# An inner Strassen product in the first gate/up pass, joined W_down sums, and the second LayerNorm spread over more units

## The chip, the cores and the metric

The kernel runs on one core of one Trainium2 chip. The metric is the device time of one execution in microseconds; several executions are taken and the median is given, with the lowest and highest. Most executions of one kernel agree within 0.3%. A profile is one execution under the hardware profiler, and its span is about 1.8 us shorter than the time of the same run.

One warning for reading small differences. The first 44 us of a run hang on loads from memory, and in the profiles quoted here the point where TensorE starts its unbroken work (43.7 to 46.0 us) differs by over 2 us from run to run with the same code up to there. The change is of that size. So beside the times I use the **length of the first pass**, from its first matmul to the first matmul of the stage behind it, read in each profile.

## The reference, cut to what matters

```python
h  = x + A(layernorm(x), wqkv, wo)                  # linear attention, 2048 tokens, width 1024
h2 = h + B(layernorm(h), W_gate, W_up, W_down)
# B: F = 3584
gate = relu(x @ W_gate);  up = x @ W_up             # [2048,1024] @ [1024,3584]
return (gate * up) @ W_down                         # [2048,3584] @ [3584,1024]
```

## The kernel before

The second half runs twice, for 1024 tokens each time: a gate/up pass of 14 units, then the W_down product. A unit is one gate or one up block: 2 column blocks of W (u = 0, 1), each 256 wide, times all 1024 tokens. Products are added up in banks of PSUM (`ps` in the profile); to read a finished bank out is called an evacuation here. A unit is computed by a Strassen-Winograd scheme: of the 2x2 blocks of W and of the activations, seven products P1 to P7 instead of eight, each of four 128-row matmuls of 512 columns. Even units ("gate") end in relu, odd ones ("up") multiply into the gate's result. The sums of weight blocks (T1 to T4, "G") are made on VectorE, the copies from bank to bank ("fork": one product feeds two outputs) on ScalarE.

```python
def ffn_unit(n, fill, mid):                 # first pass
    ...
    def p1(u):
        prod(u, BA[u], w_blk(u, 0, 0), a_blk(0, 0), True, "P1")     # 4 matmuls of 512
        ident_act(bank(BB[u]), bank(BA[u]), ...)                     # fork 1, ScalarE
    def p2(u):
        prod(u, BA[u], w_blk(u, 1, 0), a_blk(1, 0), False, "P2")
        evac(0, 0, u, BA[u], "h11")
    p1(0); p1(1)
    fillin(1)                                # one of the weight sums of the next unit
    ... P5, P6, P2, P7, P3 ...
    for u in range(2):
        prod(u, BB[u], t_blk(u, 3), a_blk(1, 1), False, "P4")
        evac(0, 1, u, BB[u], "h21")
    if n < NPAIR - 2:
        load_w_next(); load_w_next()

def ffn_unit2(n, pre, wina, winb):          # second pass: P1 and P5 by an inner Strassen
    def sub(dst, bdst, w, x, start, name):   # one of seven small products
        for kk in range(2):
            mm(dst, w[0](kk), x[0](kk), ...)                         # 2 matmuls of 256
    ...

def wd_sums(q):                             # W_down sums: four of 128x512 for each of 14 row pairs
    add(0, wb(0, 1), wb(0, 0), ...); add(2, wb(1, 1), wb(0, 1), ...)
    add(1, wb(1, 1), wsum[:, k, 0, :], ...); add(3, wb(1, 0), wsum[:, k, 1, :], ...)

# end of the attention stage: weights of units 0 and 1 are loaded from its loop
    if t in (4, 5, 18, 19):
        load_w_next()
load_w_next(); load_w_next()                 # unit 2
```

The second LayerNorm of the later 1024 tokens (three ScalarE steps for each of eight tiles) is fitted into eight of the first pass's units, three steps a unit.

Of the kernel before, what the change touches and what calls it, by code (L numbers as in the profile page):

```python
# [132 lines left out]
def bass_sequential_preLN__linear_attn_block__glu_gated_reglu__prompt_kernel(  # L133
# [71 lines left out]
    with es:  # L205
# [105 lines left out]
        m5r = RW[:, (NWS - 3) * WDW:(NWS - 3) * WDW + 2 * SHB].bitcast(f32)  # L311
        sg_g = [RWG[:, x:x + 4 * WDW].bitcast(f16).rearrange("p (j m t) -> p j m t", j=4, t=SHB)
# [134 lines left out]
        B_m5r = _Buf("m5r")  # L447
        B_xr = bufs("xr_", 2)
# [73 lines left out]
        B_m5r.over = flat(B_wsum)  # L522
        for b_ in B_hnE:
            b_.over = B_o + B_oT
# [184 lines left out]
        def wd_sums(q):  # L709
            k = q % NWR  # L710

            def wb(r, h):
                return wraw[:, k, r, h * NW:(h + 1) * NW]

            def add(o, in0, in1, reads):
                PL.add("dve", lambda e: e.tensor_tensor(out=wsum[:, k, o, :], in0=in0, in1=in1, op=ALU.subtract),
                       reads=reads, writes=[B_wsum[k][o]], name="WT%d_%d" % (o, q))

            add(0, wb(0, 1), wb(0, 0), [B_wraw[k]])
            add(2, wb(1, 1), wb(0, 1), [B_wraw[k]])  # L720
            add(1, wb(1, 1), wsum[:, k, 0, :], [B_wraw[k], B_wsum[k][0]])
            add(3, wb(1, 0), wsum[:, k, 1, :], [B_wraw[k], B_wsum[k][1]])
            dma(sl_ws[k], t_v[:, q % 2, :, q // 2, :], wsum[:, k].rearrange("p o (h c) -> p (o h) c", c=HNW),
                "st_wt_%d" % q, reads=B_wsum[k], writes=[B_tscr[q]])
            dma(sl_rw[k], r_v[:, 0, 2 * (q % 2):2 * (q % 2) + 2, q // 2, :],
                wraw[:, k, 1, NW:2 * NW].rearrange("p (h c) -> p h c", c=HNW), "st_rw_%d" % q, reads=[B_wraw[k]],
                writes=[B_rscr[0][q]])

        def wl_sums(m):
            z = m % 2  # L730

            def wq_(k, h):
                return wsum[:, (2 * m + k) % NWR, :, h * HNW:(h + 1) * HNW], B_wsum[(2 * m + k) % NWR]

            def t(j):
                return lsum[:, :, j, :], [B_lsum[j]]

            def add(j, x, y):
                PL.add("dve", lambda e: e.tensor_tensor(out=lsum[:, :, j, :], in0=x[0], in1=y[0],
                                                        op=ALU.subtract),  # L740
                       reads=x[1] + y[1], writes=[B_lsum[j]], name="WL%d_%d" % (j, m))

            def half(i):
                if i == 0:
                    add(0, wq_(0, 1), wq_(0, 0))
                    add(2, wq_(1, 1), wq_(0, 1))
                else:
                    add(1, wq_(1, 1), t(0))
                    add(3, wq_(1, 0), t(1))
                    dma(sl_ls[0], l_v[:, 0:4, :, m, :], lsum, "st_wl_%d" % m, reads=B_lsum, writes=[B_lscr[m]])  # L750
            def wr(k, h):
                return wraw[:, (2 * m + k) % NWR, 1, NW + h * HNW:NW + (h + 1) * HNW], [B_wraw[(2 * m + k) % NWR]]

            def addw(j, x, y):
                PL.add("pool", lambda e: e.tensor_tensor(out=lsw[:, z, j, :], in0=x[0], in1=y[0], op=ALU.subtract),
                       deps=[PL.prog["pe"][-1]], reads=x[1] + y[1], writes=[B_lsw[z][j]], name="WM%d_%d" % (j, m))

            def t_(j):
                return lsw[:, z, j, :], [B_lsw[z][j]]

            def last():
                addw(3, wr(1, 0), t_(1))
                if m == NM - 1:
                    load_wd_next()
                    load_wd_next()
                dma(sl_lw[z], l_v[:, 4, :, m, :], lsw[:, z], "st_wm_%d" % m, reads=B_lsw[z], writes=[B_wscr[m]])
                for q in (2 * m + NWR, 2 * m + NWR + 1):
                    if q < NPAIR:
                        load_wraw(q)
            raw = [lambda: addw(0, wr(0, 1), wr(0, 0)), lambda: addw(2, wr(1, 1), wr(0, 1)),  # L770
                   lambda: addw(1, wr(1, 1), t_(0)), last]
            return [lambda: half(0), lambda: half(1), raw]

# [617 lines left out]
        def hh_sums(q):  # L1391
            f1, f2 = 2 * q, 2 * q + 1
            PL.add("dve", lambda e: e.tensor_tensor(out=D1[:, q, :], in0=hh[:, f1, SBW:2 * SBW],
                                                    in1=hh[:, f2, SBW:2 * SBW], op=ALU.add),
                   reads=[B_hh[f1][1], B_hh[f2][1]], writes=[B_D1[q]], name="D1_%d" % q)
            PL.add("dve", lambda e: e.tensor_tensor(out=hh16[:, f1, SBW:2 * SBW], in0=hh[:, f1, 0:SBW],
                                                    in1=hh[:, f1, SBW:2 * SBW], op=ALU.subtract),
                   reads=[B_hh[f1][0]], writes=[B_hh[f1][1]], name="D3_%d" % q)

# [11 lines left out]
        def w_inner1(n):  # L1411
            z = n % 2
            i = (2 * n) % NWG
# [11 lines left out]
            g = B_g1[z]  # L1425
# [6 lines left out]
        def x_inner(first=False):  # L1432
            xs, bxs = (xs1, B_xs1) if first else (xs5, B_xs5)
# [36 lines left out]
        def ffn_unit(n, fill, mid):  # L1470
            Lg = n * 2
            up = n % 2
            iw = [(Lg + u) % NWG for u in range(2)]
            kt = [(Lg + u) % NTR for u in range(2)]
            f0 = 2 * (n - up)
            BA, BE, BB, BC_ = [0, 1], [2, 3], [4, 5], [6, 7]
            if up:
                BB, BC_ = BC_, BB

            def H(k, t, u):  # L1480
                return hh[:, f0 + 2 * u + k, t * SBW:(t + 1) * SBW], B_hh[f0 + 2 * u + k][t]

            def H2(k, t):
                return hh[:, f0 + k:f0 + k + 3:2, t * SBW:(t + 1) * SBW], [B_hh[f0 + k][t], B_hh[f0 + 2 + k][t]]

            def fillin(n_):
                for _ in range(n_):
                    if fill:
                        fill.pop(0)()

            def go(fs):
                for f_ in fs:
                    f_()

            def a_blk(k, t):
                return (lambda kk: hnT[:, k * KH + kk, t * SBW:(t + 1) * SBW]), B_hnT[t * STB:(t + 1) * STB]

            def s_blk(i):
                return (lambda kk: Ssum[:, i, kk, :]), [B_S[i]]

            def w_blk(u, k, h):
                return (lambda kk: wring[:, iw[u], k * KH + kk, h * P:(h + 1) * P]), [B_w[iw[u]]]

            def t_blk(u, j):
                return (lambda kk: Tring[:, kt[u], j, kk, :]), [B_T[kt[u]][j]]

            def prod(u, b, st_, mov, start, name):
                (sf, sr), (mf, mr) = st_, mov
                for kk in range(KH):
                    mm(bank(b), sf(kk), mf(kk), start and kk == 0, kk == KH - 1, sr + mr, B_bank[b],  # L1510
                       "%s%s_0_%d" % (name, "gu"[up], n), skip=True)

            def evac5(k, t, u, src, bsrc, tmp, btmp, name):
                d, db = (tmp[:, u, :], btmp[u]) if up else H(k, t, u)
                PL.add("dve", lambda e: e.tensor_tensor(out=d, in0=src, in1=ftmp[:, u, :], op=ALU.add),
                       reads=[bsrc, B_s5[u]], writes=[db], name=name)

            def fin5(k, t, tmp, btmp, name):
                d, db = H2(k, t)
                if up:  # L1520
                    PL.add("dve", lambda e: e.tensor_tensor(out=d, in0=d, in1=tmp, op=ALU.mult), reads=btmp, writes=db,
                           name=name)
                else:
                    PL.add("act", lambda e: e.activation(out=d, in_=d, func=ACTF.Relu), reads=[], writes=db, name=name)

            def evac(k, t, u, b, name):
                d, db = H(k, t, u)
                if up:
                    PL.add("dve", lambda e: e.tensor_tensor(out=d, in0=bank(b), in1=d, op=ALU.mult),
                           reads=[B_bank[b]], writes=[db], name=name)  # L1530
                else:
                    ident_act(d, bank(b), [B_bank[b]], [db], name, func=ACTF.Relu)

            def p1(u):
                prod(u, BA[u], w_blk(u, 0, 0), a_blk(0, 0), True, "P1")
# [53 lines left out]
        def ffn_unit2(n, pre, wina, winb):  # L1589
# [127 lines left out]
            if n > 0:  # L1717
                p2()
# [788 lines left out]
```

## Time and profile before

| | before |
|---|---|
| time, median (lowest to highest) | 719.08 us (719.01 to 719.67) |
| profile span | 717.7 us |
| first gate/up pass | 227.18 to 396.39 = 169.21 us |
| period of a first-pass unit | 12.087 us, 56 matmuls |
| period of a second-pass unit | 11.69 us, 40 matmuls of 512 and 28 of 256 |

TensorE is the bound throughout, at full clock, and the first pass has no gap: 784 matmuls x 0.21583 us are the 169.21 us.

### The profile page before, as it was taken

What the parts mean: (1) busy time and instruction counts of PE and PEld (TensorE: products, weight loads), DVE (VectorE), ACT (ScalarE), POOL (GpSimd) and SP (SyncE); (2) the same over time, 40 slices, a digit from 0 to 9 for tenths busy, and PEclk for the clock granted to TensorE, in tenths of its full rate; (3) what the DMA queues carried; (4) which work ended last, traced back from release to release, by engine and by line L of the source; (5) the groups of instructions that cost most, each with busy time, mean ns of one, the idle gap of its engine ahead of it and who ended that gap; (6) DMA issues with size and microseconds to landing.
All of it is one profiled execution on the core that took longest, in us unless ns stands there. A gap on an engine that the chain in (4) does not pass through costs nothing.

```text
span 717.7 us, 13021 instructions
## 1 busy us (share of the span) xinstructions
PE 708.3 (99%) x4923; PEld 387.4 (54%) x4979; DVE 597.5 (83%) x1010; ACT 384.1 (54%) x679; POOL 109.1 (15%) x178
## 2 busy tenths in 40 slices
PE   9999999999999999999999999999999999999998
PEld 4344444444444444444444568865555555547887
DVE  6988867799776889889888787888888888988885
ACT  4877666764841456687756102036766667643010
POOL 3221100000360103422321002320000000000331
PEclk9999999999999999999999999999999999999999
DMA  9843244015998797999999999995343534267996
GB/s 296 260 86 92 38 128 162 13 31 97 209 217 243 236 273 233 275 310 304 298 276 268 308 265 310 321 243 155 96 132 105 160 101 135 82 203 246 321 321 186
DMA packets 195102, 144.18 MB, mean 201 GB/s; under 512 B 53984, under 2 KB 172512, under 8 KB 195040
## 3 DMA queue, kind: packets, MB, share of 16 engines
q1 hardware_dynamic: 190048, 138.77, 66.3%
q0 software_dynamic: 4032, 3.67, 3.5%
q10 hardware_dynamic: 960, 0.92, 0.4%
q8 instruction: 39, 0.64, 0.4%
q14 instruction: 23, 0.19, 0.1%
HBM read 98.76 MB, written 32.51 MB: 183 GB/s over the span
## 4 chain that ended last, share of the span: by engine, by line
PE 93%; DVE 3%; DMA 2%; issue 1%; SPq 1%; DVEq 0%
PE ps L777 93%; DMA RE<-in_A_x_dram 1%; DMA RAB<-in_A_wqkv_dram 1%; DVE RW L1001 1%; DMA RAB<-RXH 1%; DVE RC L1001 1%; SPq L573 1%; DVE RWG L1026 0%; DVE st L791 0%; DVE RE L865 0%; DVE RE L1856 0%; DVE RX L1114 0%; DVE RXH L903 0%; DVE RX L862 0%; DVE RWG L1796 0%
## 5 line engine op out<-in xcount | busy, mean ns | idle before, releaser
L782 ACT ACTIVATE ps<-ps 128x512 f32<-128x512 f32 (+1 forms) x233 | 122.2, 531 | 199.8 <-PE ps L777 171.3
L777 PE MATMUL ps<-RC,RO 128*128 128x512 f16 x616 | 143.0, 370 | 0.0
L777 PEld LDWEIGHTS ps<-RC,RO 128*128 128x128 f16 x616 | 60.2, 98 | 58.0
L777 PE MATMUL ps<-RH,RWG 128*128 128x512 bf16 (+1 forms) x395 | 91.0, 365 | 0.1
L777 PE MATMUL ps<-RC,RWG 128*128 128x512 f16 x320 | 79.1, 380 | 0.3 <-ACT RE L990 0.3
L782 ACT ACTIVATE RE<-ps 128x512 f32<-128x512 f32 (+3 forms) x85 | 49.3, 596 | 39.1 <-PE ps L777 28.9
L777 PEld LDWEIGHTS ps<-RH,RWG 128*128 128x128 bf16 x396 | 38.6, 98 | 40.9 <-ACT ps L782 0.2
L777 PE MATMUL ps<-RH,RO 128*128 128x512 bf16 (+1 forms) x228 | 57.3, 380 | 1.5
L1865 POOL DMA_DIRECT2D out_dram<-RX x20 | 17.9, 1256 | 260.6 <-DVE RX L1856 218.3
L777 PE MATMUL ps<-RW,RE 128*128 128x512 bf16 x243 | 56.6, 380 | 0.8 <-issue 0.2
L777 PE MATMUL ps<-RW,RAB 128*128 128x256 f16 (+3 forms) x358 | 52.5, 300 | 0.2
L777 PEld LDWEIGHTS ps<-RC,RWG 128*128 128x128 bf16 (+1 forms) x320 | 30.0, 98 | 37.4 <-ACT ps L782 6.2
L777 PE MATMUL ps<-RAB 128*128 128x512 bf16 (+2 forms) x236 | 49.5, 348 | 0.2 <-issue 0.2
L777 PEld LDWEIGHTS ps<-RW,RAB 128*128 128x128 f16 (+1 forms) x362 | 35.3, 98 | 14.5
L1856 DVE TENSOR_TENSOR RE<-ps,RE 128x512 f32<-128x512 f32 x44 | 30.2, 686 | 15.1 <-PE ps L777 12.4
L1381 DVE TENSOR_TENSOR RO<-RWG 128x1024 f16<-128x1024 bf16 x54 | 36.9, 684 | 4.5 <-DMA RWG<-in_B_W_up_dram 4.5
L777 PEld LDWEIGHTS ps<-RW,RE 128*128 128x128 bf16 x256 | 23.9, 98 | 28.0 <-DVE RXH L1279 0.4
L777 PEld LDWEIGHTS ps<-RH,RO 128*128 128x128 f16 (+1 forms) x256 | 24.4, 98 | 27.2 <-ACT RX L782 1.5
L1629 DVE TENSOR_TENSOR RE<-ps,RE 128x512 f32<-128x512 f32 (+1 forms) x28 | 26.8, 958 | 14.2 <-PE ps L777 14.1
L1381 DVE TENSOR_TENSOR RO<-RWG,RO 128x1024 f16<-128x1024 bf16 x54 | 37.0, 685 | 0.5
L782 ACT ACTIVATE RAB<-ps 128x512 bf16<-128x512 f32 (+1 forms) x49 | 32.0, 654 | 5.9 <-PE ps L777 5.6
L777 PEld LDWEIGHTS ps<-RAB 128*128 128x128 bf16 (+1 forms) x238 | 23.1, 98 | 20.3 <-ACT RAB L921 0.3
(188 smaller groups left out, 1224.8 us busy)
## 6 DMA issues: line engine op xcount, KB each, us to landing
RWG<-in_B_W_gate_dram SPq DMA_DIRECT2D x28, 512.0 KB, 5.9
RWG<-in_B_W_up_dram SPq DMA_DIRECT2D x28, 512.0 KB, 5.1
RW<-l_scr SPq DMA_DIRECT2D x20, 448.0 KB, 5.8
RW<-in_B_W_down_dram SPq DMA_DIRECT2D x14, 512.0 KB, 5.3
t_scr<-RW SPq DMA_DIRECT2D x14, 512.0 KB, 4.5
l_scr<-RX SPq DMA_DIRECT2D x7, 1024.0 KB, 5.8
RE<-l_scr SPq DMA_DIRECT2D x15, 448.0 KB, 4.6
RE<-in_A_x_dram SPq DMA_DIRECT2D x23, 256.0 KB, 3.4
```

Source lines behind the costliest of these rows:

```text
L573: return PL.add(eng, lambda e: e.dma_start(dst_ap, src_ap), reads=reads, writes=writes, slot=slot, name=name)
L777: lambda e: e.matmul(out_ap, lhsT, rhs, start=start, stop=stop, skip_group_check=skip),
L782: PL.add("act", lambda e: e.activation(out=dst, in_=src, func=func), reads=reads, writes=writes, name=name)
L1001: PL.add("dve", lambda e: e.tensor_tensor(out=t(j)(d), in0=in0(d), in1=in1(d), op=ALU.subtract), reads=reads, writes=[btw[j]], name="%s%d" ...
L1381: PL.add(eng, lambda e: e.tensor_tensor(out=tb(j, u), in0=f0(u), in1=f1(u), op=ALU.subtract), reads=[B_w[i + x] for x in r] + ([B_T[k + x] ...
L1629: PL.add("dve", lambda e: e.tensor_tensor(out=dst, in0=in0, in1=in1, op=op), reads=reads, writes=writes, name=name)
L1856: PL.add(eng, lambda e: e.tensor_tensor(out=dst, in0=in0, in1=in1, op=op), reads=reads, writes=writes, name=name)
L1865: PL.add("pool", lambda e: e.dma_start(dst, src, accum_op=ALU.add), reads=[bsrc], writes=[B_hscr[st]], slot=sl, name="acc_%d_%d" % (st, dh))
```

## The change

The intent is to stream fewer columns. The first product of 12 of the 14 first-pass units is itself done by seven products instead of eight, one unit ahead. To find room for the extra sums on VectorE and the copies on ScalarE, other work is joined and spread. The core of the diff:

```diff
+        def inner1(ps_, n):
+            return 0 < n < NPAIR and (ps_, n) != (0, 2)
-        def ffn_unit(n, fill, mid):
-        def ffn_unit2(n, pre, wina, winb):
+        def ffn_unit(ps_, n, pre, wina, winb, mid=(), lna=(), lnb=(), tail=()):
+            nxt = inner1(ps_, n + 1)
+            plain = not inner1(ps_, n)
...
+            if ps_ == 0:
+                if plain:
+                    p1()                     # P1 and its forks in the unit itself
+                go(late21)                   # last output of the unit before
+                p5(0); p2(); run(mid, 1); out11(0); go(lna); p5(1)
+                go(wina); p6(0); r15(); p6(1); run(mid, 1)
...                                           # r15, R2..R7: P1 of the NEXT unit, 14 matmuls of 256
             prod(0, BB[0], t_blk(0, 3), a_blk(1, 1), False, "P4")
             if nxt:
                 sub(rX, B_r, Gr(3), Ar(1, 1), False, "R4")
                 for u in range(2):
                     fk1(u, BC_)              # the forks of the next unit's P1
...
-        def wd_sums(q):                      # eight instructions of 512 for two row pairs
+        def wd_pair(q):                      # three: one of 2048, two of 1024
+            def one():
+                add(wsum[:, :, 0:4:2, :], wraw[:, :, :, NW:2 * NW], ...)
...
-        load_w_next()
-        load_w_next()
         for q in range(NWR):
             load_wraw(q)
+        load_w_next()
+        load_w_next()
...                                           # LayerNorm: two steps a unit, units 1 to 12
```

The two outputs of an evacuation also become one instruction of 1024 elements, and in up units ScalarE first copies two of the outputs so that VectorE multiplies from SBUF.

## The prediction

> **What bounds the kernel now.** I read four views, in this order. First the page, for which engine is full:
>
> ```profile
> PE 708.3 (99%) x4923; PEld 387.4 (54%) x4979; DVE 597.5 (83%) x1010; ACT 384.1 (54%) x679; POOL 109.1 (15%) x178
> ...
> PEclk9999999999999999999999999999999999999999
> ...
> PE 93%; DVE 3%; DMA 2%; issue 1%; SPq 1%; DVEq 0%
> ```
>
> TensorE is busy all the time at the full granted clock and is 93% of the chain that ended last. Busy does not yet mean without gaps, so next I read the chain of waits in order of time, in both gate/up passes:
>
> ```profile
> 225.67 12.03 PE ps L777 x55
> ...
> 382.79 12.04 PE ps L777 x55
> ...
> 485.99 11.64 PE ps L777 x67
> ```
>
> The chain runs through TensorE without a break. It is cut at the same place of every unit, so the distance of two cuts is the period of a unit: from 225.67 to 394.88 there are 14 units of the first pass, 12.087 us each. A first-pass unit is 2 x 7 products of 4 matmuls of 512 columns, 56 in all: 12.087 / 56 = 0.2158 us each. The table of windows, one row for a unit, shows what runs beside that:
>
> ```profile
> 274.01:286.10 12.09, 12.04 (x55) 5.46 (x56) 11.85 (x20) 7.71 (x12) 3.39 (x6) 1.00 0.64 202
> 286.10:298.19 12.09, 12.04 (x56) 5.48 (x56) 9.83 (x20) 10.03 (x17) 4.12 (x6) 1.00 1.11 294
> ...
> 533.25:544.94 11.69, 11.64 (x69) 6.65 (x69) 10.49 (x20) 7.78 (x15) 0.00 (x0) 1.00 0.48 137
> 544.94:556.63 11.69, 11.64 (x69) 6.65 (x69) 10.40 (x19) 7.86 (x15) 0.00 (x0) 1.00 0.40 111
> ```
>
> Columns: stretch, its length, then busy time of PE, PEld, DVE, ACT, POOL, the clock, DMA share, GB/s. The two upper rows are a pair of first-pass units (VectorE 21.68 of 24.17 us, 90%), the two lower ones a pair of second-pass units, which already have **two** inner Strassens each: 11.69 us, with VectorE at 20.89 of 23.38, 89%. So there is no TensorE gap in the first pass to win back; time falls only by streaming fewer columns, and the second pass is a working example of it.
>
> **What the Trainium skill says.** "TensorE: Matmul & The Clock Gate", section "Back-to-back issue gap", gives N/2.4 + 2.5 ns between warm matmuls: 215.8 ns at 512 columns and 109.2 at 256. The trace agrees with the first (215.8 measured above). The second follows from it: a second-pass unit is 40 matmuls of 512 and 28 of 256, 40 x 0.2158 + 28 x 0.1092 = 11.69 us, exactly the period above. "SBUF — State Buffer", section "Who interferes with whom": a VectorE instruction with two SBUF inputs and a GpSimd instruction that reads SBUF take turns at a shared interface. The trace agrees; these are the level-two W_down sums:
>
> ```profile
> L739 DVE TENSOR_TENSOR RX<-RW x12: 684/1151/1158, 251.6 to 373.0; 128x1024 f16<-128x1024 f16 x12
> L739 DVE TENSOR_TENSOR RX<-RW,RX x12: 682/688/693, 256.7 to 378.3; 128x1024 f16<-128x1024 f16 x12
> ```
>
> Minimum, median and maximum ns: the same size takes 684 alone, and 1151 when it lies over the GpSimd sums of the same weights. "VectorE: DVE Perf Modes", section "The perf-mode tier table", has 1224 ns for a bf16 tensor_tensor of 2048 elements; this trace has 1215 for 2048, 688 for 1024, 420 for 512 and 292 for 256, so about 0.15 us is fixed and joining two instructions saves that.
>
> **The change, part by part.**
>
> *TensorE.* In 12 of the 14 first-pass units (not units 0 and 2) the first product of both halves, 8 matmuls of 512, becomes 14 of 256, made one unit ahead. 8 x 0.2158 - 14 x 0.1092 = 1.727 - 1.529 = 0.198 us. The same from the two passes: (12.087 - 11.690) / 2 = 0.199. Times 12: **-2.38 us**. The order of instructions confirms it: 96 fewer wide matmuls and 168 more narrow ones. A steady unit should take 11.89 us.
>
> *VectorE, for a pair of units (gate, up).* Added: weight sums of the inner product, 0.42 + 2 x 0.29 = 1.00 a unit, and one joint sum in PSUM of 0.70 a unit: +3.40. Saved: the four 0.68 evacuations of a unit become two of 1.225: -0.57 a pair. The four PSUM multiplies of an up unit (0.685) become two of 0.686 after ScalarE copies: -1.37. The eight 0.42 W_down sums become 1.215 + 2 x 0.688 = 2.59: -0.77. The level-two sums fall from 2 x 0.998 + 2 x 0.688 to 2.59: -0.78. The hidden-state sums go from 4 x 0.42 to 2 x 0.688: -0.30. Sum -0.39: 21.3 us of a pair of 23.78, 90%. The GpSimd sums move from the up unit to the gate unit, where up to four of them can each cost VectorE the 0.47 us seen above: 21.3 to 23.2, **90 to 97%**. Beside TensorE, but close.
>
> *ScalarE, for a pair.* Added: three copies of 256 columns a unit, 1.13; in the up unit, 2 x 0.59 + 1.02 of copies: +4.45 a pair. LayerNorm goes from three steps of about 1.23 us a unit in eight units to two a unit in twelve: -2.47 a pair there. 17.75 + 4.45 - 0.17 - 2.47 = 19.6 of 23.78, 82%. Off the path by amount; its order matters more.
>
> *Where lateness would reach TensorE.* I laid a steady unit out by hand, time 0 at its first P5 matmul. P7 ends at 7.75, and the fourth product may overwrite its bank at 9.9. In an up unit VectorE first has 12 other instructions, about 8.1 us by the start-to-start distances of the trace (0.60 for 1024 elements, 0.70 where one needs the one before). So the P7 evacuation runs from 8.1 to 9.3, 0.6 us before TensorE asks for the bank. In the gate unit there is about 0.5 us of backlog at its start and 0.5 to 0.9 of GpSimd collisions, and the evacuation ends at about 9.3 to 9.6. The copies into the next unit's banks end near 12.4, before the second half of P2 needs the bank at 13.5. I chose to count **zero** for steady units, as the second pass gets by with similar figures, and 0.15 us for all of them together as a reserve.
>
> *Opening.* Unit 0 now needs the inner weight sum of unit 1. In the trace VectorE waits there for a load:
>
> ```profile
> 233.13 0.69 DVE L1381 TENSOR_TENSOR RO<-RWG 128x1024 f16<-128x1024 bf16 x1 [4.47 <-DMA RWG<-in_B_W_up_dram]
> ```
>
> The load lands at 233.1, so the sum is ready at about 233.6. TensorE, which starts unit 0 at 227.2 and has 28 wide and 2 narrow matmuls first, asks for it at 233.45. I count +0.15.
>
> *Transfers.* Same bytes; the raw W_down loads go ahead of unit 2's weights, and unit 2 is left plain, so nothing is due earlier than it lands. The late LayerNorm is spread over twelve units, which lowers the DMA share (1.11 in the upper table). Counted 0.
>
> Sum: 719.08 - 2.38 + 0.15 + 0.15 = 717.0; I put 716.9.
>
> **Rivals.** (1) *VectorE becomes the bound of the first pass.* For it: 97% at worst, in-order, and the 0.6 us margin. Against it: -0.39 us of work per pair before collisions, and the second pass at 89% without a gap. If each of the five or six steady pairs lost 0.5 to 1 us, the gain is gone: 717 to 720. (2) *The path through ScalarE.* A LayerNorm step of 1.23 us now lies between a P2 evacuation and the P5 copy, and the next fork waits behind it; a step whose input is late would hold everything behind it. Against it: ScalarE has 2 us spare in each unit and loads run a step and a half ahead. If it bites, 0.2 us in ten units: 719. (3) *The weights land late.* The inner sums need a weight at the start of the unit before its use, and VectorE blocks on it. Against it: loads are issued nearly two units ahead and land in about 6 us. For it: DMA share over 1 in some units. Would cost 1 to 3 us, once or twice. (4) *The gain is hidden anyway.* Not so: nothing else ends beside TensorE in this pass.
>
> **Range and chances.** No gap at all gives 716.7; single runs of before spread over 0.7 us, so the low end is 715.9. Half of the gain lost, and a little more, gives the high end 718.6. Faster by 2% would need 14 us, six times what is taken away; slower by 2% would need a stall of over 1 us in every unit. Within 2%: 0.98.
>
> **What would show it right or wrong.** Right: the cuts of the chain in the first pass lie 11.89 us apart from unit 3 to 12, about 13.6 at units 0 and 2 and 10.4 at 1 and 13; VectorE at 21.3 to 23.2 us a pair; the later stages unchanged. Wrong by rival 1: longer periods in alternate units, with TensorE or its weight loads waiting for VectorE at a fourth product. By rival 2: waits for ScalarE at P6 or P2. By rival 3: VectorE waiting for a weight transfer at the head of a unit. What would upset the sum is a mis-sized collision with GpSimd, as that is the one term taken from a different overlap than the new order has.

## The result, and the profile after

The changed kernel took **717.93 us** in the median (717.65 to 719.65, 4 runs), the kernel before 719.38 in the same rounds. The ratio is 0.9984, 95% interval 0.9966 to 1.0002. A ratio is the mean time of one kernel's fast runs over that of the other's of the same rounds, so it is not quite the ratio of the medians. A second timing, on another chip with five rounds, gave 0.998 (0.9968 to 0.9993). So the kernel is faster by about 0.2%, within 2%; the interval of the first timing alone still includes no change, that of the second does not. In the two profiles all of the gain lies in the first pass: the stretch from the start of TensorE's unbroken work to the pass took 182.99 us before and 182.91 after, and from the end of the pass to the end of the span it is 321.3 and 321.4.

Of the page of the profile after, the lines of the whole:

```profile
PE 706.1 (99%) x4995; PEld 394.8 (55%) x5051; DVE 602.8 (84%) x964; ACT 404.5 (57%) x729; POOL 110.2 (15%) x178
...
PE 94%; DVE 2%; DMA 2%; issue 1%; ACT 0%; DVEq 0%; ACTq 0%; SPq 0%
```

TensorE is as full as before with 2.2 us less of busy time. The chain of waits in the first pass of the changed kernel (start, length, what) tells more:

```profile
226.24 1.10 issue
227.33 1.22 DVE RXH L1297
228.56 0.34 DVE RX L1455
...
228.96 4.39 DMA RWG<-in_B_W_up_dram
233.35 0.02 issue
233.37 0.43 DVE RAB L1433
233.81 0.05 issue
233.85 5.58 PE ps L795 x30
...
311.06 11.84 PE ps L795 x61
322.90 0.05 issue
322.95 11.84 PE ps L795 x61
```

Two readings. In the steady part the cuts lie 11.89 us apart, ten units in a row. (A cut is no wait: it is the place where one matmul record of each unit is missing, 14 in the pass, before as after. In e9's profile, which lacks none there, the chain has no such cut.) But at the head of the pass the chain leaves TensorE: it goes through a load of unit 1's weights that lands at 233.35 and through the inner weight sum on VectorE (L1433). Before, the same stretch was TensorE alone. Why the load is late shows in the queue of SyncE, which issues the loads one after the other:

```profile
228.58 0.33 SPq L587 DMA_DIRECT2D out_dram<-RXH  x1
228.96 0.45 SPq L587 DMA_DIRECT2D RWG<-in_B_W_up_dram  x1
```

The load stands behind a store of an attention tile that VectorE (L1297 in the chain) finishes only at 228.55. TensorE's own timeline there:

```profile
233.12 0.38 PE L795 MATMUL ps<-RH,RWG 128*128 128x256 bf16 x2
233.85 0.39 PE L795 MATMUL ps<-RX,RAB 128*128 128x256 f16 x2 [0.35 <-DVE RAB L1433]
```

The two R1 matmuls start at 233.12 and take 0.22 of TensorE's stream (a matmul's own length overlaps the next), so R5 could start at 233.34; it starts at 233.85. That is a stop of **0.51 us**. The pass as a whole is 227.07 to 394.52 = 167.45 us, 1.76 shorter than before.

The table of windows for a pair of steady units, an up and a gate unit (stretch, length, then busy time of PE, PEld, DVE, ACT, POOL, clock, DMA share, GB/s):

```profile
311.01:322.90 11.89, 11.84 (x61) 6.07 (x62) 10.97 (x16) 9.56 (x18) 1.72 (x4) 1.00 1.03 286
322.90:334.79 11.89, 11.84 (x61) 6.08 (x62) 11.55 (x16) 8.98 (x16) 2.80 (x5) 1.00 0.99 300
```

VectorE is busy 22.52 of 23.78 us, 95%, ScalarE 18.54. The GpSimd sums now lie in the gate unit and there meet VectorE, as one sees in VectorE's timeline beside GpSimd's:

```profile
327.61 1.19 DVE L1399 TENSOR_TENSOR RO<-RWG 128x1024 f16<-128x1024 bf16 x1
328.71 3.11 DVE L731 TENSOR_TENSOR RW<-RW 128x2048 f16<-128x2048 bf16 x3
...
332.95 1.21 DVE L1533 TENSOR_TENSOR RAB<-ps,RE 128x1024 bf16<-128x1024 f32 x1
```

```profile
327.57 0.67 POOL L774 TENSOR_TENSOR RAB<-RW 128x256 f16<-128x256 bf16 x1 [3.90 <-PE ps L795]
330.61 0.67 POOL L774 TENSOR_TENSOR RAB<-RW 128x256 f16<-128x256 bf16 x1 [2.36 <-PE ps L795]
```

The weight sum that starts at 327.61, just behind a GpSimd instruction, takes 1.19 us instead of 0.68, and the second GpSimd sum lengthens one of the three W_down sums by 0.45. Still the evacuation at 332.95 ends at 334.16, and TensorE overwrites its bank from 334.84 on: 0.68 us of lead.

### The profile page after: what moved, and what is told of

The parts are those of the page before. It is cut to its first block, busy times and chain, and to the rows that moved or that the text cites. A ratio compares the mean times of both kernels' runs of the same rounds, so it can differ in the third digit from the quotient of the medians.

```text
span 715.9 us, 13148 instructions
## 1 busy us (share of the span) xinstructions
PE 706.1 (99%) x4995; PEld 394.8 (55%) x5051; DVE 602.8 (84%) x964; ACT 404.5 (57%) x729; POOL 110.2 (15%) x178
## 4 chain that ended last, share of the span: by engine, by line
PE 94%; DVE 2%; DMA 2%; issue 1%; ACT 0%; DVEq 0%; ACTq 0%; SPq 0%
PE ps L795 94%; DMA RWG<-in_B_W_up_dram 1%; DMA RAB<-RXH 1%; DMA RE<-in_A_x_dram 0%; DVE RWG L1044 0%; DVE st L809 0%; PE ps L957 0%; DVE RE L883 0%; DVE RE L1794 0%; DVE RX L1132 0%; DVE RXH L1297 0%; DVE RW L1019 0%; DVE RX L880 0%; DVE RXH L921 0%; PE ps L936 0%
## 5 line engine op out<-in xcount | busy, mean ns | idle before, releaser
L800 ACT ACTIVATE ps<-ps 128x512 f32<-128x512 f32 (+1 forms) x257 | 129.6, 516 | 189.7 <-PE ps L795 145.3
L795 PE MATMUL ps<-RC,RO 128*128 128x512 f16 x616 | 147.0, 369 | 0.0
L800 ACT ACTIVATE RE<-ps 128x512 f32<-128x512 f32 (+3 forms) x106 | 63.8, 627 | 32.2 <-PE ps L795 18.1
L795 PE MATMUL ps<-RH,RWG 128*128 128x512 bf16 (+1 forms) x347 | 77.5, 348 | 0.1
L1533 DVE TENSOR_TENSOR RE<-ps,RE 128x1024 bf16<-128x1024 f32 (+1 forms) x42 | 44.0, 1047 | 18.2 <-PE ps L795 18.1
L795 PEld LDWEIGHTS ps<-RH,RWG 128*128 128x128 bf16 x348 | 34.0, 98 | 35.2 <-ACT ps L800 0.2
L1533 DVE TENSOR_TENSOR RAB<-ps,RE 128x1024 bf16<-128x1024 f32 x28 | 34.2, 1223 | 7.6 <-PE ps L795 7.0
L1533 DVE TENSOR_TENSOR RAB<-RAB,RE 128x1024 bf16<-128x1024 bf16 x56 | 37.2, 685 | 2.8 <-ACT RE L800 2.4
L1399 DVE TENSOR_TENSOR RO<-RWG 128x1024 f16<-128x1024 bf16 x54 | 39.4, 729 | 0.0
L1545 ACT ACTIVATE RAB<-RAB 128x1024 bf16<-128x1024 bf16 x28 | 29.5, 1053 | 17.4 <-DVE RAB L1533 17.4
```

The source lines that it names most:

```text
L795: lambda e: e.matmul(out_ap, lhsT, rhs, start=start, stop=stop, skip_group_check=skip),
L800: PL.add("act", lambda e: e.activation(out=dst, in_=src, func=func), reads=reads, writes=writes, name=name)
L1399: PL.add(eng, lambda e: e.tensor_tensor(out=tb(j, u), in0=f0(u), in1=f1(u), op=ALU.subtract), reads=[B_w[i + x] for x in r] + ([B_T[k + x] ...
L1533: PL.add("dve", lambda e: e.tensor_tensor(out=dst, in0=in0, in1=in1, op=op), reads=reads, writes=writes, name=name)
L1545: PL.add("act", lambda e: e.activation(out=d, in_=d, func=ACTF.Relu), reads=[], writes=db, name=name)
```

## The experiments

All kernels compute the right result. The edits are against the changed kernel. "Pass" is the length of the first pass in the run's profile.

| run | edit | pass us | time us (median) | ratio to before (95%) |
|---|---|---|---|---|
| c_changed | none | 167.49 | 718.33 | 0.998 (0.9968 to 0.9993) |
| e1_plain | no inner product | 171.04 | 721.0 | 1.002 (1.0006 to 1.0034) |
| e2_early | unit 1's weights 8 steps earlier | 166.92 | 718.73 | 0.9994 (0.9982 to 1.0007) |
| e3_thirteen | as e2, unit 2 inner too | 167.28 | 720.95 | 1.0013 (1.0 to 1.0025) |
| e4_narrow | W_down sums narrow | 168.13 | 718.42 | 0.9981 (0.9964 to 0.9997) |
| e5_dve1 | +0.6 us VectorE a unit | 170.36 | 720.23 | 1.0012 (0.9997 to 1.0027) |
| e6_dve2 | +1.2 us VectorE a unit | 177.01 | 727.35 | 1.011 (1.0095 to 1.0125) |
| e7_lnburst | LayerNorm 3 steps a unit | 167.73 | 717.9 | 0.9984 (0.9968 to 0.9999) |
| e8_eleven | unit 1 plain too | 167.17 | 717.43 | 0.9971 (0.9958 to 0.9985) |
| e9_mid | unit 1's weights 2 steps earlier | 166.93 | 716.82 | 0.9971 (0.9958 to 0.9983) |
| e10_thirteen | 13 inner units, sums moved | 169.02 | 719.27 | 0.9997 (0.9984 to 1.0009) |
| e11_order | as e1, copy ahead of forks | 169.84 | 720.03 | 1.0017 (1.0001 to 1.0033) |

My theory was: what pays is the 2.38 us of columns; what was given back is a stop at the opening; the joined sums and the spread LayerNorm only make room. The rivals: these other parts save time themselves; VectorE has become the bound; ScalarE's order matters; weights come late.

**The control**, in one job with e1, e2 and e3.

> The changed kernel once more, as the partner of the next three on one chip. Both theories: first gate/up pass (first P1 matmul of unit 0 to the first matmul of the first W_down product) 167.45 us as in its first profile, 0.51 us of it a TensorE stop at the first R5 of unit 0; steady units 11.89 us apart.

Pass 167.49, with the same periods as in the first profile. So the pass repeats to 0.04 us where the span moved by 0.6. The pass has a scatter of its own, though: by the unrounded start times the stop at the opening was 0.52 us in the first profile and 0.57 here, and in e4 to e7, whose edits leave that load and the sum behind it alone, it was 0.63, 0.78, 0.43 and 0.75. So differences of 0.3 us between passes are read from the stops below, not from the length alone.

**No inner product at all.**

```diff
-            return 0 < n < NPAIR and (ps_, n) != (0, 2)
+            return ps_ == 1 and 0 < n < NPAIR
```

> The changed kernel with every first-pass unit plain: no inner Strassen there; wide W_down sums, joint evacuations and spread LayerNorm stay. Theory (only the streamed columns pay, the rest makes room): pass 169.2 us as in the kernel before, steady units 12.09, span 717.6, within 0.1% of before. Rival (the wide sums, joint evacuations and the spread LayerNorm themselves save time): pass stays under 168 us and the time about 1 us below before.

Both were wrong: the pass took 171.04 us, 1.83 **longer** than in the kernel before with the same 784 matmuls. The rival falls at once: the rest of the change saves nothing by itself, it costs. VectorE's timeline shows where; this is the head of a gate unit:

```profile
328.58 0.69 DVE L1533 TENSOR_TENSOR RAB<-RAB,RE 128x1024 bf16<-128x1024 bf16 x1 [1.90 <-ACT RE L800]
```

VectorE stands still 1.90 us for a ScalarE copy that it multiplies with; over units 2 to 13 that is 25.1 us in 12 waits. In a plain unit ScalarE does the two forks of P1 first and that copy behind them. With the inner product the forks lie at the end of the unit before, and in the steady part of the changed kernel VectorE waited for TensorE only. Later in such a unit the evacuation comes late, and in four gate units TensorE waits 0.30 us for it. The other 0.62 us of the 1.83 are 14 small gaps, for which see e11.

**The same with the copy first.**

```diff
-                if plain:
-                    p1()
                 go(late21)
                 late21.clear()
+                if plain:
+                    p1()
```

> As e1 (all first-pass units plain), but with the last output of the unit before copied ahead of the two forks of P1 instead of behind them. Theory (e1 lost 1.8 us because ScalarE does the two forks first, VectorE waits 2 us for the copy it multiplies with, and its evacuation of P7 is late): VectorE's wait at the head of gate units shrinks and the pass falls from 171.0 to about 169.2 to 169.8. Rival (plain units are slow in the new order for another reason, such as the joint evacuations): pass stays at 170.5 or more.

The pass fell by 1.20 us to 169.84, just over the range I gave, and TensorE no longer stopped for VectorE at all in it. VectorE's waits for the copies halved, to 13.7 us in 6 waits. So the order of forks and copy is most of what made e1 slow; 0.63 us stays over that of before. The matmuls' start times show where: one gap of 0.045 us in each of the 14 units, at the start of P7, whose first weight load waits for ScalarE's second fork:

```profile
330.91 0.55 PEld L795 LDWEIGHTS ps<-RC,RO 128*128 128x128 f16 x4 [0.36 <-ACT ps L800]
```

The kernel before has P2 between P6 and P7, and a unit that makes the next unit's inner product has two of its small products between the two halves of P6; neither has the gap. The changed kernel has it in units 1 and 13 alone, which make none. The times of e11 scatter (719.3 to 722.14).

**Unit 1's weights earlier.** First by eight steps of the attention loop, then by two.

```diff
-            if t in (4, 5, 18, 19):
+            if t in (4, 5, 10, 11):        # e2
+            if t in (4, 5, 16, 17):        # e9
```

> The changed kernel with the two weight loads of unit 1 issued at attention steps 10 and 11 instead of 18 and 19. Theory (the 0.51 us TensorE stop in unit 0 comes from the load that lands at 233.4): the stop goes, pass 166.95 us, span 715.4. Rival (the stop is VectorE's queue, which only reaches the inner sum then): the stop and the pass of 167.45 stay. A cost on the attention side, if the early loads disturb its transposes, would show before 227 us.

The stop went and the pass took 166.92, as the theory said. But the time did not follow. From the start of TensorE's unbroken work to the pass it took 184.43 us (44.84 to 229.27) against 182.92 (44.79 to 227.71) in the control: 1.5 us lost in the attention stage. Its chain of waits:

```profile
208.31 0.58 SPq L587
...
209.00 3.04 SPq L591
...
217.39 4.85 DMA RE<-RE
222.24 0.14 issue
222.37 5.34 PE ps L795 x24
```

The chain runs through SyncE's queue (SPq): the weight load at 208.31 is followed by a transpose instruction that keeps the queue 3.04 us, later transposes are issued late, and the last but one (RE<-RE) lands at 222.24, where TensorE waits for it. In the control the same transpose goes out at 214.41 instead of 217.39. The two loads take 0.6 us of the queue each, and the transposes just behind them 2.31 and 3.04 us, against 1.25 and 1.24 there. Why these two take longer no run separates; that the place of the loads decides is shown by the next run.

> The changed kernel with the two weight loads of unit 1 issued two attention steps earlier (16 and 17 instead of 18 and 19), after the last transposes of the attention output. Theory (the stop in unit 0 is the late load; what e2 lost before 227 us was its loads getting in the way of transposes): no stop in unit 0, pass 166.95 us, and the pass starts no later than in the changed kernel (227 to 227.8). Rival (any earlier load costs the attention stage as much): pass start at 228.5 or later.

With the loads behind the last transpose both are had: pass 166.93, and 182.97 us from the start of the unbroken work (43.69) to the pass. R5 now starts at 232.93, 0.22 us after R1, and TensorE waits for nothing in the pass. The chain of waits of the whole run has one TensorE piece over attention, first pass, first W_down product and second pass:

```profile
43.69 631.43 PE ps L795 x4454
```

(That the piece is in one is no proof by itself: this profile lacks no matmul record there, and those of e8 and e11, complete there too, also have one piece, e11's in spite of its 14 gaps.)

The time is 716.82 us, ratio 0.9971: faster than before by 0.29% and the best version together with e8. Against the changed kernel's 0.998 (other chip, so each against its own runs of before) that is 0.09%, 0.65 us, and the pass accounts for 0.56 of it. The intervals of the two ratios overlap, so it is the pass and not the time that tells e9 from the changed kernel.

**Unit 1 plain.**

```diff
+            return 0 < n < NPAIR and (ps_, n) not in ((0, 1), (0, 2))
```

> The changed kernel with unit 1 plain too: 11 inner units, and unit 0 no longer needs unit 1's weights for TensorE. Theory: the 0.51 us stop goes, one unit's 0.198 us is lost, pass 167.45 - 0.51 + 0.20 = 167.15 us. Rival (the stop moves to unit 1 or to the plain unit's forks, as in e1): pass 167.5 or more.

Pass 167.17, forecast 167.15. One inner product fewer costs 0.2 us and saves the 0.51 us stop. Its trace has no stop at the opening. So the sum of both sizes is confirmed from another side, with a stop of the size of the first profile's.

**Thirteen inner units.** Two attempts. Both also load unit 2's weights in the attention loop.

```diff
-            return 0 < n < NPAIR and (ps_, n) != (0, 2)
+            return 0 < n < NPAIR
-                        (tail if q == 0 else winb).extend(wd_pair(q))
+                        (tail if q in (0, 2) else winb).extend(wd_pair(q))     # e10 only
```

> As e2, with unit 2's weights early too and unit 2 also with the inner Strassen, 13 units in all. Theory: 680 x 0.2158 + 182 x 0.1092 = 166.6 us plus 0.1 of small gaps, pass 166.7, span 715.2, 0.35% below before. Rival (unit 1 has no room for another inner sum, or its weights land late): a stop in unit 1 or 2 gives the 0.2 us back, pass 166.9 to 167.5.

> Loads of units 1 and 2 at steps 16 to 19, 13 inner units, and the W_down sums of unit 2 moved behind its evacuations, as unit 0 has them. Theory (e3's 0.6 us stop in unit 2 came from those sums standing in front of an evacuation): no stop, pass 166.7 us, 2.5 below before, time 0.35% below before. Rival (VectorE has no room in units 1 to 3): stop stays, pass 167.2 or more.

Both missed, and both times the pass lay in the rival's range. In e3 TensorE stops once, 0.6 us, for VectorE in unit 2, and the attention stage loses 2.4 us (185.31 from the start of unbroken work to the pass). I put the stop down to the W_down sums in front of an evacuation. Three VectorE instructions of that unit are also longer by about 1.4 us together beside GpSimd, and no run separates the two. e10 moved the sums behind the evacuation, and the pass grew to 169.02 by two stops. The first, 1.29 us in unit 3, is the sums in their new place: from 263.99 on VectorE works without a pause, and the evacuation for which TensorE waits ends at 275.77:

```profile
274.56 1.21 DVE L1533 TENSOR_TENSOR RE<-ps,RE 128x1024 bf16<-128x1024 f32 x1
```

The second, 1.03 us in unit 4, goes through a load, as the chain shows: the sums at 263.99 end late, their stores and then the next raw W_down load go out late through SyncE, the load lands at 283.14, and VectorE and then TensorE wait for it:

```profile
263.99 1.23 DVE RW L731
...
277.23 5.92 DMA RW<-in_B_W_down_dram
283.14 0.03 issue
...
283.34 1.24 DVE RW L731
```

So leaving unit 2 plain was no oversight of the change: VectorE and the loads behind its sums have little room there. Whether another order would fit a thirteenth inner unit stays open.

**How near VectorE is to being the bound.** The first weight sum is done twice or three times (with the same result).

```diff
-                        winb.append(tq[0])
+                        winb += [tq[0]] * 2        # e5;  * 3 in e6
```

> The changed kernel with one VectorE instruction of 0.6 us more in each first-pass unit (the first weight sum is done twice). Theory: VectorE 23.6 of 23.78 us a pair, the lead of 0.7 us is nearly used up, units stay at 11.89 to 12.0; pass 167.5 to 168.7. Rival 1 (VectorE already bounds): 0.6 us a unit, pass about 175.

> The changed kernel with two such VectorE instructions more in each first-pass unit: 24.8 us of VectorE work for a pair of 23.78. Both theories now expect TensorE to wait: about (24.8 + 0.3 - 23.78) / 2 = 0.6 us a unit, pass 173 to 177, and the waits at the fourth product and the forks after it. If nothing grows, the lead was mis-sized by over 1 us a unit.

The first cost 2.87 us, more than the 0 to 1.2 us I gave; the second 9.5 us, at the top of its range. All stops but the one at the opening lie at a fourth product, as e6 was expected to show. In e5 they are not even: five units stop, by 0.33 to 0.97 us, the others not at all. In the steady part of e6 a gate unit stops by 1.1 us (once 1.45) and an up unit by 0.4. Over the five steady pairs, units 3 to 12, e5 adds 1.2 us of VectorE work a pair and loses 0.27 in the mean, e6 adds 2.4 and loses 1.58. A margin of 0.8 to 0.9 us a pair, about 0.4 a unit, fits both. The lead of 0.68 us that one reads off a timeline is not all usable. I argue that part of it goes back to VectorE's own gaps (an instruction that needs the one before starts 0.72 us after it instead of 0.60), but no run separates that. In any case the changed kernel is not bound by VectorE: in its steady part TensorE never waited.

**The narrow W_down sums.**

```diff
-                add(wsum[:, :, 1, :], wb(1, 1), wsum[:, :, 0, :], B_wraw + bs(0), bs(1))
+                for k in range(2):
+                    add(wsum[:, k, 1, :], wraw[:, k, 1, NW:2 * NW], wsum[:, k, 0, :], ...)
...     # likewise the first and third, and the first of the level-two sums
```

> The changed kernel with the W_down sums of the first pass narrow again (8 + 4 instructions a pair instead of 3 + 3): VectorE gets about 0.9 us more work a pair, 22.4 to 23.3 of 23.78. Theory (VectorE has 0.7 to 0.9 us of lead before TensorE asks for a bank): it is just kept or just used up, units stay at 11.89 or the gate unit grows by at most 0.1 us; pass 167.4 to 168.0. Rival 1 (VectorE is the bound in disguise): every pair grows by 0.5 us or more, pass over 170.

Steady units stayed at 11.89 us. The pass took 168.13, just over the range, by one stop in unit 2, and its chain names the reason:

```profile
241.54 2.76 DVE RW L731 x8
...
248.37 7.58 DMA RWG<-in_B_W_up_dram
255.97 0.44 DVE RAB L1436
```

The eight narrow sums end later at the opening, the stores behind them hold SyncE's queue, and the weights of unit 3, issued behind those, land at 255.95, when VectorE already waits for them. So the joined sums matter once, through a load, and not through VectorE's steady load. (The stop in unit 2 is 0.56 us; the other 0.1 is the opening's scatter.)

**The LayerNorm back in eight units.**

```diff
-                    if q > 0 and ln_q:
+                    if q > 2 and ln_q:
...
+                        f_, t2 = ln_q.pop(0)
+                        tail.append(f_)
```

> The changed kernel with the late LayerNorm in eight units at three steps a unit, as before, instead of twelve at two. ScalarE gets 1.23 us more in each of those units, about 11.0 of 11.89. Theory (ScalarE has over 1.5 us spare in a unit and the spreading is only a precaution): pass within 0.2 us of 167.45. Rival 2 (the spreading is needed): the forks for the next unit come late, TensorE stops at P2 or P6 in those units, 0.3 us or more each, pass over 169.

Pass 167.73, which is 0.28 us over the 167.45 and so just outside the 0.2 I gave. The profile's granted clock of 0.998 does not explain it, since within the pass it was 1.00. The start times do: the stop at the opening was 0.75 us in this profile, 0.23 longer than in the first, and a few gaps of 5 to 11 ns in the eight units make 0.05 together. No unit stops at P2 or P6 for 0.3 us. So the spreading is worth 0.05 us at most in these profiles; ScalarE has the room either way.

## Why the prediction was right

- **TensorE, -2.38 us.** Right. Steady units lie 11.89 us apart; units 1 and 13 took 10.62 us and unit 2 13.40, against the 10.4 and 13.6 of the forecast. Counting 688 matmuls of 512 and 168 of 256 at the durations of the prediction gives 166.83 us for a pass without a stop; e9, which has none, took 166.93, and the two gaps at P7 (see e11) are the difference.
- **Opening, +0.15 us.** The mechanism was right, the size was not: 0.51. The load landed at 233.35 in place of 233.1, and TensorE, which started the pass 0.11 us sooner, was there at 233.34 in place of 233.45. I had taken the landing from the other kernel to a tenth, for a difference of two times that are both free to move. By the 0.43 to 0.78 us of the other profiles it moves by 0.35.
- **Reserve for steady units, +0.15.** About 0.1 of small gaps, as in e9, and none of them in a steady unit.
- **Sum.** A gain of 2.38 - 0.51 - 0.10 = 1.77 us, and the pass is shorter by 1.76. In time it was 1.2 us by the first ratio and 1.4 by the second; the profiles of the two kernels differ by 1.8. The forecast of 716.9 was 1.0 us low, inside the range; 0.4 of that is the opening, and the medians of before move by up to 0.5 from job to job.
- **VectorE 90 to 97%.** 95% in the pair shown. The collisions with GpSimd cost 0.45 to 0.50 us each, as estimated from the 1151 ns row; of the four sums of the pair shown two collide, since here only those that start before a VectorE instruction hold it up. Without them the pair has 21.6 us, against 21.3.
- **ScalarE 19.6 us a pair.** 18.5, and which term was too large is not traced; its place in the order was no problem with the inner product and was one without it (e1), in a way that I had not thought of: not the LayerNorm steps but the forks in front of a copy.
- **Rivals.** VectorE as the bound: no, but the margin is 0.4 us a unit (e5, e6). ScalarE's LayerNorm: no (e7). Weights late: yes, once, at the opening, which I had kept as a small separate term.
- **What I had not seen.** I took the saving in columns as a bare subtraction from the old time. In fact the new schedule without the inner product would have cost 1.83 us more than the old (e1); the inner product also moves two forks out of the way. Of the 1.83 us, 1.2 is the forks' place and 0.6 the gaps at P7, which the inner product also fills. The prediction's number came out because in 12 of 14 units the forks are moved and the gaps filled, which I had not reckoned with: that part is luck.

## What to carry to other kernels

Where TensorE has no gap, only fewer streamed columns shorten the time, and a part of the same kernel that already does it gives the saving exactly: the period of its unit. Check the first use of each new operand separately, at the stage's opening, and move its load to the first free place behind the transfers that the stage before still needs: here two steps gained the half microsecond and eight steps lost three times as much. Build the new order without the new product as well: only e1 showed what the order costs. For effects under 0.5%, time a stage by its own first and last matmul; whole-run times carry the scatter of the start. Then look for the stops in it, as the stage's length has some scatter too.

## What the Trainium skill lacked or had wrong

- "TensorE: Matmul & The Clock Gate", section "Back-to-back issue gap", says that in a real stream of weight loads and matmuls the sustained spacing at 512 columns is about 131 ns and that N/2.4 + 2.5, the gap of a single matmul, over-counts there. Here the formula holds: 784 matmuls, each with its own weight load, lie 215.8 ns apart, and those of 256 columns 109.2 ns.
- "SBUF — State Buffer", section "SBUF: two separate sides", has the shared pair as an exclusive lock: whichever instruction starts first has it to its end, and the other is fully blocked. The traces agree nearly. VectorE sums of 684 ns that started under a GpSimd sum lost 0.45 to 0.50 us (1151 ns before, 1190 after), and those that started before one lost nothing. What the page lacks: the loss was 0.14 us less than what the GpSimd sum had still to run, 0.59 to 0.64 us by the profile, in every one of the 17 cases in the first pass of the two kernels.
- No page that I used gives the cost of a place in SyncE's queue: two weight loads put in front of transposes cost the stage 1.5 us (e2), behind the last transpose nothing that shows (182.97 us against 182.92, e9).
